# GpSimd takes over half of the scaling of the first-layer weight blocks

## The chip, the cores and the metric

The kernel runs on one core of a Trainium2 chip. A core has five engines that run side by side, each through its own fixed list of instructions: TensorE (PE in the profile, with its weight loads as PEld) multiplies matrices into PSUM; VectorE (DVE), ScalarE (ACT) and GpSimd (POOL) work on elements, 128 partitions at a time; SyncE (SP) issues most of the DMA transfers. An instruction starts when the one ahead of it on its engine has been issued and the semaphores that it waits for have been raised. The metric is the time of one execution on the device, in microseconds (us).

## What is computed

Attention with normalised queries and keys, for 8 sequences of 448 tokens and 12 heads of 64, then a layer that takes the largest of three products, and an output layer:

```python
def rmsnorm(x, g):
    rms = np.sqrt(np.mean(x * x, axis=-1, keepdims=True) + 1e-06)
    return x / rms * g
q_n, k_n = (rmsnorm(q, g_q), rmsnorm(k, g_k))
scores = (1.0 / np.sqrt(64)) * np.matmul(q_n, k_n.transpose(0, 1, 3, 2))
attn = softmax(scores)                      # rows over the keys
x = (attn @ v), heads side by side          # 3584 x 768
h = np.maximum(np.maximum(x @ w1, x @ w2), x @ w3)
out = h @ w_out                             # all weights 768 x 768
```

The weights arrive as 64-bit floats.

## The kernel before

**Products in two halves.** Most matrix products are done in f16 with each operand as a sum of an upper and a lower half: upper = f16(x), lower = f16(x - upper). Three matmuls (`TERMS`: upper by upper, upper by lower, lower by upper) give nearly the precision of f32. So that the halves use the range of f16, each operand is scaled first by a power or a bound.

**The weights.** `w1`, `w2`, `w3` are cut into 18 blocks of 128 x 768 (six column groups `ft`, three matrices `j` each), `w_out` into six. A block is loaded as raw 64-bit words (`load_raw`, two buffers) and goes through these steps, each in a later beat of the program:

- `rebias` (L188): ScalarE multiplies the upper words by a constant.
- `decode` in three stages on VectorE (L196, L200, L205): the bits of a 64-bit float become those of an f32, in place in `f`.
- when the three blocks of an `ft` are decoded, `bound_in` finds their largest magnitude (L170, then two small matmuls and a reduction in `largest`), and `scale` computes `w_up`, a column with UP / bound in each partition.
- `upper` and `lower` then split each block: this is where the change is.

`f` is no separate tile. `plain(w_sb, n)` is slot n + 1 of `w_sb` seen as f32, while the two f16 halves of block n go into slot n. So the halves of block n lie where the f32 of block n - 1 was.

**The order.** Nothing is scheduled by a tool: each engine runs its instructions in the order in which the program issues them. The program is a loop over 48 pairs of heads, `g`, with 12 beats each. A beat issues one piece of the scores, the softmax, the product with the values and the next pair's normalisation, then a few matmuls of the feed-forward layers (`thirds`), and at its end `tick()` issues what was put off to this beat by `later(beats, work)`. One first-layer block is taken up every 4 beats. `upper` of a block comes 2, 6 or 10 beats after the bound is known, `lower` 2 beats behind it. The output blocks (`bound_out`) are split in another way, which stays.

**What stands around it on the engines.** On GpSimd: the squares of queries and keys (L365), the inverse root mean squares (L383, L387), the scaling of keys and queries (L419, L423, L394, L406) and, from pair `PLAIN` = 6 on, the lower halves of queries and keys (L440) and the scaling and splitting of values (L517, L531). On ScalarE: the exponentials (L579), their preparation (L570), the copies of transposed weights (L611) and further evictions. On VectorE: the row maxima (L562), the sums of squares (L372), the lower halves of the attention weights (L665) and the decoding. The first layer's matmuls are at L732, the output layer's at L796.

Of the kernel before, what the change touches and what calls it, by code (L numbers as in the profile page):

```python
# [12 lines left out]
AF = mybir.ActivationFunctionType  # L13
ALU = mybir.AluOpType
# [25 lines left out]
def qknorm_attention_maxout_ffn_kernel(  # L40
# [35 lines left out]
    nc = tc.nc  # L76
# [36 lines left out]
    def later(beats, work, last=False):  # L113

        due.setdefault(clock[0] + beats, ([], []))[last].append(work)
# [31 lines left out]
    def largest(column, done, gaps):  # L147


        top = sb.tile([1, 1], F32, name="top", bufs=2)  # L150
        box = []

        def turn():
            box.append(ps_m.tile([P, 512], F32, name="marks", tag="m"))
            nc.tensor.matmul(box[0][0:1, 0:P], column, ident, start=True, stop=True)

        def reduce():
            nc.vector.tensor_reduce(top, box[0][0:1, 0:P], axis=AX, op=ALU.max)

        def spread():  # L160
            box.append(ps_m.tile([P, 512], F32, name="most", tag="m"))
            nc.tensor.matmul(box[1][:, 0:1], ones, top, start=True, stop=True)

        at = 0
        for gap, work in zip(gaps, (turn, reduce, spread, lambda: done(box[1][:, 0:1]))):
            at += gap
            later(at, work)

    def row_largest(dst, src):
        nc.vector.tensor_reduce(dst, src, axis=AX, op=ALU.max, apply_absolute_value=True)  # L170
# [4 lines left out]
    w_sb = const.tile([P, NFT * NJ + 1, 2, NCT * P], F16, name="w_sb")  # L175
# [55 lines left out]
    def plain(t, n):  # L231
        return t[:, n + 1].rearrange("p a n -> p (a n)").bitcast(F32)
# [17 lines left out]
    def bound_in(ft):  # L250
        most = sb.tile([P, 1], F32, name="most", bufs=2)
        n = ft * NJ + 1
        row_largest(
            most, w_sb[:, n:n + NJ].rearrange("p n a f -> p (n a f)").bitcast(F32)
        )

        def scale(bound):
            top, up = w_most[:, ft:ft + 1], w_up[:, ft:ft + 1]
            nc.vector.tensor_scalar(
                out=top, in0=bound, scalar1=LEAST, scalar2=None, op0=ALU.max  # L260
            )
            nc.vector.reciprocal(up, top)
            nc.vector.tensor_scalar(
                out=up, in0=up, scalar1=UP, scalar2=None, op0=ALU.mult
            )

            def upper(n, f):
                nc.scalar.activation(f, f, AF.Copy, scale=up)
                nc.scalar.copy(w_sb[:, n, 0], f)

            def lower(n, f):
                nc.gpsimd.tensor_tensor(
                    out=w_sb[:, n, 1], in0=f, in1=w_sb[:, n, 0], op=ALU.subtract
                )

            for j in range(NJ):
                n = ft * NJ + j
                f = plain(w_sb, n)
                later(2 + 4 * j, lambda n=n, f=f: upper(n, f), True)
                later(4 + 4 * j, lambda n=n, f=f: lower(n, f), True)  # L280

        largest(most, scale, (3, 2, 4, 1))
# [578 lines left out]
    for i, src in enumerate((g_q, g_k)):  # L861
        nc.scalar.dma_start(
            out=gains[:, i], in_=src.rearrange("(o d) -> o d", o=1).broadcast_to([P, D])
# [205 lines left out]
```

## Time and profile before

| | us |
|---|---|
| median of 3 timed runs | 1098.78 |
| lowest and highest | 1097.26, 1098.79 |
| span of the profiled execution, first to last instruction | 1101.6 |
| PE busy in that span | 1018.6 (92%) |
| DVE busy | 757.8 (69%) |
| ACT busy | 772.1 (70%) |
| POOL busy | 702.4 (64%) |
| first to last scaling of a first-layer block (L268) | 64.9 to 196.8 |
| first to last matmul of the first layer (L732) | 163.4 to 1073.9 |

The profile gives for the profiled execution its span only, and no time beside it. Shares of the whole span say little here, since the program has a stage in which weights are prepared and a longer one in which they are used. The views are read by stretches of time therefore. A group of instructions is a line with its engine and operation, how many there were, their busy time in us and the mean of one in ns, then the idle time of the engine just before them and what ended it. A row of the timeline is start and duration in us, engine, line, operation, output and inputs. The windows view gives for a stretch its length, then busy time (and instructions) of the engines, the granted clock of TensorE, the share of the DMA engines and GB/s.

### The profile page before, as it was taken

How to read it: one execution, taken by the hardware profiler on the slowest of the kernel's cores; microseconds unless marked ns; L12 is line 12 of the kernel's file. 1: busy time of each engine (PE TensorE's matmuls, PEld its weight loads, DVE VectorE, ACT ScalarE, POOL GpSimd, SP SyncE). 2: the span in 40 equal slices, each digit the busy share in tenths (PEclk: the TensorE clock that was granted, in tenths of full speed). 3: DMA queues.
4: the chain of work that ended last, by engine and by line, in shares of the span. 5: the costliest groups of instructions: out<-in, count | busy, mean ns of one | idle time of the engine just before them, and what ended most of it. 6: DMA issues, size and time to landing. Idle time of an engine off the chain costs nothing. (4 is left out here: it accounts for less than half of the span.)

```text
span 1101.6 us, 18390 instructions
## 1 busy us (share of the span) xinstructions
PE 1018.6 (92%) x6168; PEld 501.9 (46%) x6168; DVE 757.8 (69%) x1390; ACT 772.1 (70%) x1767; POOL 702.4 (64%) x805
## 2 busy tenths in 40 slices
PE   4678768988999999999999999999999999999998
PEld 2334333434444455444544454444444454445555
DVE  3899988888667676677677776777677766762210
ACT  4599887767868678687877777778777787773001
POOL 5477988856767767678677686776867677610000
PEclk9687868998989999999999999999999999999999
DMA  5554466856787679877888789787877798563002
GB/s 149 165 164 152 129 180 137 179 115 125 151 166 149 134 151 172 160 148 133 176 155 149 136 169 175 141 151 150 170 146 143 145 166 153 106 106 73 1 1 58
DMA packets 426654, 152.29 MB, mean 138 GB/s; under 512 B 372928, under 2 KB 422336, under 8 KB 426560
## 3 DMA queue, kind: packets, MB, share of 16 engines
q1 hardware_dynamic: 425888, 150.75, 66.8%
q8 instruction: 48, 0.79, 0.3%
q10 hardware_dynamic: 672, 0.38, 0.1%
q14 instruction: 46, 0.38, 0.1%
HBM read 51.97 MB, written 11.01 MB: 57 GB/s over the span
## 5 line engine op out<-in xcount | busy, mean ns | idle before, releaser
L732 PE MATMUL acc<-xt,w_sb 128*128 128x448 f16 x2592 | 520.6, 356 | 0.6 <-ACT m L742 0.6
L732 PEld LDWEIGHTS <-w_sb 128*128 128x128 f16 x2592 | 245.1, 99 | 262.9 <-issue 53.1
L562 DVE TENSOR_REDUCE sc<-sc 112x2 f32<-112x896 f32 x192 | 209.7, 1092 | 47.8 <-PE sc L553 46.6
L579 ACT ACTIVATE sc<-sc,nm,down 112x448 f32<-112x448 f32 x336 | 234.2, 697 | 11.2
L655 ACT ACTIVATE pp<-sc,rs 112x448 f16<-112x448 f32 x336 | 194.8, 632 | 48.5 <-ACT sc L579 40.4
L665 DVE SCALAR_TENSOR_TENSOR pp<-sc,rs,pp 112x448 f16<-112x448 f32 x336 | 212.9, 675 | 3.4 <-ACT pp L655 2.9
L387 POOL TENSOR_TENSOR ri<-ri,half_neg 128x7 f32<-128x7 f32 x96 | 154.2, 1606 | 8.0
L553 PE MATMUL sc<-kt,qt 64*112 64x448 f16 x1008 | 133.7, 371 | 27.1 <-DVE pp L665 23.6
L570 ACT ACTIVATE nm<-sc,down 112x2 f32<-112x2 f32 x192 | 50.7, 264 | 149.5 <-DVE sc L562 148.2
L796 PE MATMUL acc<-wo_sb,ht 128*128 128x384 f16 x864 | 151.4, 330 | 1.4 <-DVE ht L756 0.8
L761 POOL COPY hx<-ht 128x128 f16<-128x128 f16 x48 | 15.5, 323 | 197.7 <-DVE ht L756 191.7
L796 PEld LDWEIGHTS <-ht 128*128 128x128 f16 x864 | 82.0, 99 | 67.5 <-issue 14.5
L703 PE MATMUL av<-pt,vp 128*64 128x448 f16 x1008 | 108.3, 356 | 0.0
L553 PEld LDWEIGHTS <-qt 64*112 64x112 f16 x1008 | 55.0, 128 | 96.9 <-issue 56.4
L648 DVE TENSOR_SCALAR rs<-sc 112x2 f32<-112x2 f32 x168 | 26.6, 158 | 94.7 <-ACT sc L579 94.7
L440 POOL TENSOR_TENSOR kp<-kn,kp 128x512 f16<-128x512 f32 x42 | 50.0, 1190 | 58.9 <-ACT kp L434 58.9
L703 PEld LDWEIGHTS <-vp 128*64 128x64 f16 x1008 | 49.6, 108 | 56.0 <-issue 30.4
L718 DVE SCALAR_TENSOR_TENSOR xt<-av,xt 128x448 f16<-128x448 f32 x42 | 26.2, 625 | 71.1 <-ACT xt L717 71.1
L372 DVE TENSOR_REDUCE ss<-sq 128x7 f32<-128x448 f32 x96 | 60.9, 635 | 10.6 <-ACT sq L363 6.6
L531 POOL TENSOR_TENSOR vp<-vr,vp 128x448 f16<-128x448 f32 x42 | 43.8, 1044 | 32.2 <-ACT vp L525 32.1
L440 POOL TENSOR_TENSOR qp<-qn,qp 112x512 f16<-112x512 f32 x42 | 49.3, 1173 | 21.0 <-ACT qp L434 20.8
L517 POOL TENSOR_SCALAR vr<-vr,v_up 128x448 f32<-128x448 f32 x42 | 60.7, 1446 | 0.0
(112 smaller groups left out, 1203.1 us busy)
## 6 DMA issues: line engine op xcount, KB each, us to landing
raw<-in_moe_w_dram SPq DMA_DIRECT2D x18, 768.0 KB, 4.4
qr<-in_q_dram SPq DMA_DIRECT2D x48, 224.0 KB, 3.0
vr<-in_v_dram SPq DMA_DIRECT2D x96, 96.0 KB, 2.5
kr<-in_k_dram SPq DMA_DIRECT2D x95, 96.0 KB, 3.0
raw<-in_moe_w_out_dram SPq DMA_DIRECT2D x6, 768.0 KB, 5.1
pt<-pp SPq DMA_TRANSPOSE x168, 4.1
out_dram<-osb SPq DMA_DIRECT2D x8, 336.0 KB, 3.2
out_dram<-osb SPq DMA_DIRECT2D x8, 288.0 KB, 3.7
```

The lines of the kernel that those rows point to most:

```text
L372: nc.vector.tensor_reduce(sums[g % 2][:sq.shape[0], KQ[what]], sq, axis=AX, op=ALU.add)
L387: nc.gpsimd.tensor_tensor(out=ri, in0=ri, in1=half_neg[:, at], op=ALU.pow)
L440: nc.gpsimd.tensor_tensor(out=parts[:, 1], in0=n, in1=parts[:, 0], op=ALU.subtract)
L517: nc.gpsimd.tensor_scalar(out=vr, in0=vr, scalar1=v_up[:, g // NP:g // NP + 1], scalar2=None, op0=ALU.mult,)
L553: nc.tensor.matmul(sc[:QP, h, :S], qt[rows, qp, c], kt[rows, kp, KEYS[h]], start=n == 0, stop=n == len(TERMS) - 1,)
L562: nc.vector.tensor_reduce(sc[:QP, 0, S + 8:S + 10], sc[:QP, :, :S], axis=AX, op=ALU.max, negate=True)
L579: nc.scalar.activation(to, sc[:QP, h, :S], AF.Exp, bias=nm[:, h:h + 1], scale=down[:QP], accum_out=total,)
L655: nc.scalar.activation(pp[:, 0, h], sc[:QP, h, :S], AF.Copy, scale=rs[:, h:h + 1])
L665: nc.vector.scalar_tensor_tensor(out=pp[:, 1, h], in0=sc[:QP, h, :S], scalar=rs[:, h:h + 1], in1=pp[:, 0, h], op0=ALU.mult, op1=ALU.subtract,)
L703: nc.tensor.matmul(av[half, :S], vp[rows, group, vpart], pt[rows, 7 * wp + group], start=u == 0 and n == 0, stop=u == 3 and n == len(TERMS ...
L732: nc.tensor.matmul(acc[:, :S], wt[:, wp, c], xs[c][:, xp], start=(c == 0 and n == 0), stop=(c == NCT - 1 and n == 2),)
L796: nc.tensor.matmul(acc[:, :HW], lhs, wo_sb[:, f, wp, half * HW:(half + 1) * HW], start=(f == 0 and n == 0), stop=(f == NFT - 1 and n == 2),)
```

## The change

`upper` no longer scales the block in place. One ScalarE instruction reads the unscaled block, multiplies by `up` and writes the f16 upper half; the cast falls away. `lower` first scales the block in place on GpSimd, as (f x up) x 1.0, and then subtracts the upper half as before. The subtraction still needs a scaled `f`, which GpSimd now makes for itself.

```diff
             def upper(n, f):
-                nc.scalar.activation(f, f, AF.Copy, scale=up)
-                nc.scalar.copy(w_sb[:, n, 0], f)
+                nc.scalar.activation(w_sb[:, n, 0], f, AF.Copy, scale=up)
 
             def lower(n, f):
+                nc.gpsimd.tensor_scalar(
+                    out=f, in0=f, scalar1=up, scalar2=1.0, op0=ALU.mult, op1=ALU.mult
+                )
                 nc.gpsimd.tensor_tensor(
                     out=w_sb[:, n, 1], in0=f, in1=w_sb[:, n, 0], op=ALU.subtract
                 )
```

The file grows by two lines, so that lines behind the change have numbers two higher. GpSimd's list at the second, third and fourth block (`w_sb` is the block, `kn` and `qn` scaled keys and queries, `sq` squares, `ri` inverse root mean squares), before:

```order
L423 TENSOR_TENSOR kn_90<-kr,ri 64x64
L272 TENSOR_TENSOR w_sb<-w_sb 128x768
L394 TENSOR_TENSOR qn<-qr,ri 112x2x4x64
L365 TENSOR_TENSOR sq<-kr 128x448
L272 TENSOR_TENSOR w_sb<-w_sb 128x768
L365 TENSOR_TENSOR sq<-qr 112x512
L272 TENSOR_TENSOR w_sb<-w_sb 128x768
L383 TENSOR_SCALAR ri<-ss_87 128x7
```

and the same place now:

```order
L425 TENSOR_TENSOR kn_90<-kr,ri 64x64
L271 TENSOR_SCALAR w_sb<-w_sb,w_up 128x768
L274 TENSOR_TENSOR w_sb<-w_sb 128x768
L396 TENSOR_TENSOR qn<-qr,ri 112x2x4x64
L367 TENSOR_TENSOR sq<-kr 128x448
L271 TENSOR_SCALAR w_sb<-w_sb,w_up 128x768
L274 TENSOR_TENSOR w_sb<-w_sb 128x768
L367 TENSOR_TENSOR sq<-qr 112x512
L271 TENSOR_SCALAR w_sb<-w_sb,w_up 128x768
L274 TENSOR_TENSOR w_sb<-w_sb 128x768
L385 TENSOR_SCALAR ri<-ss_87 128x7
```

Ahead of each subtraction stands one more instruction; the rest keeps its order. ScalarE's list at one block (`pt` transposed weights, `nm` and `e` of the softmax), before:

```order
L611 COPY pt<-turned 128x3x112
L268 ACTIVATE w_sb<-w_sb,w_up 128x768
L269 CAST w_sb<-w_sb 128x768
L570 ACTIVATE nm<-sc,down 112x2
L579 ACTIVATE e,sum<-sc,nm,down 112x448 x2
```

and now:

```order
L613 COPY pt<-turned 128x3x112
L268 ACTIVATE w_sb<-w_sb,w_up 128x768
L572 ACTIVATE nm<-sc,down 112x2
L581 ACTIVATE e,sum<-sc,nm,down 112x448 x2
L613 COPY pt<-turned 128x4x112
```

The cast is gone, and the preparation of the softmax follows directly. The lists of TensorE, VectorE and SyncE are the same but for line numbers.

## The prediction

> **What bounds the kernel now.** First the page's second part, the busy tenths in 40 slices of 27.5 us.
>
> ```profile
> PE   4678768988999999999999999999999999999998
> DVE  3899988888667676677677776777677766762210
> ACT  4599887767868678687877777778777787773001
> POOL 5477988856767767678677686776867677610000
> ```
>
> From about slice 9 on, TensorE (PE) is busy nine tenths or more: it sets the pace, and the chain that ended last is made of its matmuls. In slices 2 to 7 (55 to 220 us) it is not: VectorE, ScalarE and GpSimd are all at seven to nine tenths. There the weight blocks are decoded, scaled and split, and only there does the change act: its rows run from 64.9 to 201 us. The order of the program is fixed, and the matmuls that follow fill TensorE almost completely, so what this stage loses or gains should shift the end by nearly as much.
>
> The windows view gives busy time per engine (PE, PEld, DVE, ACT, POOL), first for the whole stage, then slice by slice.
>
> ```profile
> 64.90:201.00 136.10, 107.05 (x566) 52.18 (x565) 123.23 (x169) 117.55 (x251) 116.01 (x98) 0.80 0.58 152
> 55.00:82.50 27.50, 20.58 (x116) 10.82 (x116) 25.79 (x36) 25.73 (x58) 19.97 (x17) 0.87 0.52 164
> 82.50:110.00 27.50, 22.71 (x109) 11.16 (x111) 27.04 (x30) 24.81 (x55) 21.86 (x18) 0.76 0.47 152
> 110.00:137.50 27.50, 20.95 (x121) 9.96 (x117) 26.04 (x31) 23.80 (x54) 24.75 (x22) 0.81 0.49 131
> 137.50:165.00 27.50, 16.97 (x84) 9.01 (x82) 24.24 (x40) 22.30 (x47) 24.41 (x22) 0.67 0.68 179
> 165.00:192.50 27.50, 24.48 (x127) 10.81 (x126) 22.64 (x37) 21.93 (x45) 22.34 (x21) 0.83 0.69 140
> 192.50:220.00 27.50, 26.27 (x159) 12.47 (x158) 23.68 (x42) 21.77 (x48) 25.02 (x24) 1.00 0.83 179
> ```
>
> In the stage's 136.1 us GpSimd is busy 116.0 and idle 20.1, ScalarE is idle 18.5, VectorE 12.9. None has room for much more.
>
> **The change part by part.** The groups of instructions in that window that it touches, and what GpSimd and VectorE waited for there:
>
> ```profile
> L272 POOL TENSOR_TENSOR w_sb<-w_sb 128x768 f16<-128x768 f32 x18 | 29.8, 1655 | 12.4 <-ACT w_sb L269 12.0
> L268 ACT ACTIVATE w_sb<-w_sb,w_up 128x768 f32<-128x768 f32 x18 | 17.1, 952 | 0.0
> L269 ACT CAST w_sb<-w_sb 128x768 f16<-128x768 f32 x18 | 15.0, 832 | 1.5
> POOL w_sb L272 <- ACT w_sb L269: 12.0, 5, 6.7
> POOL ri L383 <- DVE ss L372: 5.5, 6, 1.9
> DVE rs L648 <- ACT sc L579: 4.3, 5, 1.4
> DVE xt L718 <- ACT xt L717: 4.2, 5, 1.3
> ```
>
> *ScalarE.* Two instructions per block become one: a scaled read that writes f16. I price it between the two rows, 0.83 to 0.95 us, so 15.0 to 17.1 us of ScalarE go, over 18 blocks. That is not 15 us of time. VectorE is idle 12.9 us in the stage, and the two largest waits on ScalarE are 4.3 and 4.2; the most that ScalarE's relief can give is about those 8.5 us, while GpSimd and VectorE keep up.
>
> *GpSimd.* 18 new products over 128x768 f32, in place, stand right ahead of the 18 subtractions. No row shows this form with two operations at this size. The nearest rows, from the calmer stretch 229 to 1000 us:
>
> ```profile
> L517 POOL TENSOR_SCALAR vr<-vr,v_up 128x448 f32<-128x448 f32 x39 | 56.5, 1449 | 0.0
> L383 POOL TENSOR_SCALAR ri<-ss 128x8 f32<-128x8 f32 x37 | 7.3, 197 | 0.6 <-DVE ss L372 0.6
> L761 POOL COPY hx<-ht 128x128 f16<-128x128 f16 x39 | 11.3, 289 | 113.6 <-DVE ht L756 107.5 <-DMA kr<-in_k_dram 6.0
> ```
>
> L517 is the same operation on the same engine, with a scalar from a column, in place in f32, but with one product: 1449 ns for 448 elements. Taking the 197 ns of the 8-element row as the fixed part, an element costs (1449 - 197) / 440 = 2.85 ns, and 768 of them 0.197 + 760 x 0.00285 = 2.36 us. The other end is the one-input copy: (289 - 197) / 120 = 0.77 ns an element, 0.78 us for 768. Above, if each product costs what L517's does, 0.197 + 760 x 0.0057 = 4.5 us. I take 2.36, since L517 is the nearest row, and keep the ends. That is 18 x 2.36 = 42.5 us more on GpSimd (14.0 at the low end, 81 at the high).
>
> Against that row stands a rule of the Trainium skill, "GPSIMD Engine Reference", section 3.1, "Elementwise — side-by-side cycle accounting": a loop with at most two arithmetic operations per element is bound by its port at 1.03 cycles per element. By its 1.2 GHz that is an estimate of 0.66 us for 768 elements, plus what an instruction costs by itself; by it GpSimd would get about 15 us, not 42. L517 speaks against the rule here, at 2.85 ns or 3.4 cycles an element with only one product.
>
> Where these fall slice by slice follows from the busy time of L272 in the same windows:
>
> ```profile
> 55.00:82.50 27.50, 3.29 (x2) 0.87 0.52 164
> 82.50:110.00 27.50, 8.03 (x5) 0.76 0.47 152
> 110.00:137.50 27.50, 5.36 (x4) 0.81 0.49 131
> 137.50:165.00 27.50, 4.91 (x3) 0.67 0.68 179
> 165.00:192.50 27.50, 6.18 (x4) 0.83 0.69 140
> 192.50:220.00 27.50, 2.00 (x2) 1.00 0.83 179
> ```
>
> Divided by 1.655 us, these are 2.0, 4.9, 3.2, 3.0, 3.7 and 1.2 blocks. Times 2.36 and added to GpSimd's busy time: 24.7, 33.3, 32.4, 31.4, 31.2 and 27.9 us of work in slices of 27.5. The overflow is 0 + 5.8 + 4.9 + 3.9 + 3.7 + 0.4 = 18.7 us, with every idle moment of GpSimd in the last five slices filled. Its waits for VectorE's sums (5.5 us) can't all be filled, since the sums themselves depend on squares that GpSimd makes: I add 2. Of ScalarE's relief I count back 1, an estimate, for the first slice only, where GpSimd has room. The sum is 18.7 + 2 - 1, about 20 us.
>
> *The order on ScalarE.* One more thing follows from the layout: a block's f32 lies in the next block's slot. The f16 half of block n overwrites memory from which block n-1's subtraction reads, so ScalarE must wait for that subtraction. In the kernel before this wait stands ahead of the cast, one instruction behind the scaling; now it stands ahead of the only instruction, some 1 us sooner, and the subtraction ends later by the whole product. How close it is:
>
> ```profile
> 142.46 1.64 POOL L272 TENSOR_TENSOR w_sb<-w_sb 128x768 f16<-128x768 f32 x1
> 144.29 0.94 ACT L268 ACTIVATE w_sb<-w_sb,w_up 128x768 f32<-128x768 f32 x1
> 145.32 0.83 ACT L269 CAST w_sb<-w_sb 128x768 f16<-128x768 f32 x1
> ```
>
> The subtraction ends at 144.10, and ScalarE comes to the next block at 144.29: 0.19 us of slack, against 2.36 of delay. Behind the waiting instruction stand the exponentials and the evictions of the softmax, and TensorE and VectorE wait for those. So GpSimd's lag can't pile up quietly in the queue; it reaches all engines within a block. This is why I do not let the stage's end absorb it.
>
> *VectorE.* Its decode operations and GpSimd's keep each other out. At 81.83 the last decode step of a block (L205) waits through one GpSimd instruction and then through the next:
>
> ```profile
> 71.36 0.95 DVE L205 SCALAR_TENSOR_TENSOR w_sb<-raw,w_sb 128x768 uint32<-128x768 uint32 x1
> ...
> 80.94 1.64 POOL L365 TENSOR_TENSOR sq<-kr 128x448 f32<-128x448 f32 x1
> 81.83 3.17 DVE L205 SCALAR_TENSOR_TENSOR w_sb<-raw,w_sb 128x768 uint32<-128x768 uint32 x1
> 82.55 1.64 POOL L272 TENSOR_TENSOR w_sb<-w_sb 128x768 f16<-128x768 f32 x1
> 84.15 1.75 POOL L365 TENSOR_TENSOR sq<-qr 112x512 f32<-112x512 f32 x1
> L205 DVE SCALAR_TENSOR_TENSOR w_sb<-raw,w_sb 128x768 uint32<-128x768 uint32 x12 | 21.8, 1814 | 0.1
> 169.08 1.41 POOL L517 TENSOR_SCALAR vr<-vr,v_up 128x448 f32<-128x448 f32 x1
> 169.13 1.77 DVE L196 TENSOR_SCALAR wo_sb<-raw 128x768 uint32<-128x768 uint32 x1
> ```
>
> Free, L205 takes 0.95 us; its mean of 1.81 holds 0.86 of such waiting. The pair at 169 us shows that a product with one tensor input shuts VectorE out as well: L196 ends 0.41 us behind it. The new product makes GpSimd's run of 1.65 us one of about 4.0. If L205's wait grows in proportion, it is 0.86 x 4.0 / 1.65 = 2.1 us, 1.2 more per block and 22 over 18. I take this as the same 20 us seen from VectorE's side, not as more: while VectorE waits, GpSimd works. Only if the two add up do I get more (below).
>
> No transfer is moved; the DMAs of the next blocks hang on decoding and start later with it.
>
> **Sum.** 1101.6 (span) + 20 = 1121.6 us for a profiled execution. The median of the timed runs, 1098.78, is 2.8 us below the profiled span, so I predict 1119.
>
> **The rivals.**
> - *Cheap product, ScalarE decides* (15%): the product costs about 0.8 us as the copy does, its 14.0 us fit into GpSimd's 20.1 idle, and ScalarE's relief counts for 3 to 8.5 us: 1090 to 1096. For it: in the first two slices ScalarE is 90 to 94% busy. Against it: L517. It decides while GpSimd's time per block rises by less than its idle share of 20.1 / 18 = 1.1 us. The rule of the Trainium skill named above would lead to this case or the next.
> - *Cheap product, nothing gained* (17%): the same price, but L205's wait grows to 0.86 x 2.43 / 1.65 = 1.27, 7 us over 18, which eats the relief: 1096 to 1106.
> - *Middling product* (12%): as much as the two-input subtraction, 1.65 us. The same sum by slices overflows by 2.4 + 2.5 + 1.9 + 0.9 = 8 us: 1104 to 1111.
> - *The forecast* (44%): 1111 to 1131; the low end if ScalarE's relief of 8.5 counts in full, the high end if GpSimd's remaining waits do.
> - *Locks add up, or two products cost more than one* (12%): VectorE's 22 us stand beside GpSimd's 20, 1131 to 1141; at 4.5 us a product, 81 - 20 = 61 us, 1160.
>
> **How the numbers follow.** The range from 1093 to 1137 leaves out about half of the first and of the last case. About 0.2%, 2.2 us, is what a measurement of this kernel can tell from no change: faster is below 1096.6, slower above 1101. The first case gives 0.14 faster, the second splits into 0.08 same and the rest slower; with a little kept back on either side that is 0.15, 0.10 and 0.75.
>
> **What the profile of the changed kernel would show.** The price of a product, in its own group: 2.4 us carries the forecast, 0.8 a cheap-product rival. GpSimd at over 95% busy from 82 to 200 us, hardly a wait for ScalarE left. ScalarE idle ahead of its scaled cast, waiting for the subtraction of the block before. L205 above 2 us. The stage some 20 us longer, with the first layer's matmuls starting some 14 us later (the overflow up to 165 us), and nothing changed behind it. I am wrong if the product is short, or if the stage is longer and TensorE wins it back afterwards.

## The result, and the profile after

| | before | after |
|---|---|---|
| median of the timed runs, us | 1098.26 (4 runs) | 1106.49 (4 runs) |
| span of the profiled execution, us | 1101.6 | 1105.7 |

The ratio is 1.0073, with a 95% interval from 1.0057 to 1.0089: the change makes the kernel slower by 8 us. I had forecast 1119, and my range began at 1093, so the time lies inside the range and the direction is right; the 20 us of the forecast are 8. The granted clock doesn't explain the longer time: in the profiled executions its mean was 0.957 before and 0.966 after.

The page's busy tenths after the change:

```profile
PE   4687747988989999999999999999999999999998
...
DVE  4799968888767676677677766777677767762210
ACT  4587757768777778687777777777777787773001
POOL 5479999966676777767677686776867677620000
```

In slices 3 to 7 GpSimd (POOL) now has nines throughout, where it had 7 to 9 before; ScalarE (ACT) fell. From slice 10 on little has changed. The windows view of the stage and of its slices (columns as before):

```profile
64.90:201.00 136.10, 99.14 (x541) 48.99 (x540) 119.11 (x163) 99.05 (x223) 129.57 (x110) 0.82 0.53 143
82.50:110.00 27.50, 19.36 (x100) 10.07 (x99) 25.33 (x30) 20.40 (x47) 26.70 (x21) 0.75 0.49 152
110.00:137.50 27.50, 21.13 (x121) 9.59 (x122) 25.92 (x30) 21.85 (x51) 26.71 (x22) 0.87 0.45 132
137.50:165.00 27.50, 13.87 (x81) 7.96 (x77) 18.66 (x32) 17.06 (x39) 26.66 (x24) 0.75 0.48 137
165.00:192.50 27.50, 21.02 (x102) 9.32 (x104) 24.88 (x41) 20.15 (x45) 26.74 (x25) 0.88 0.79 167
```

From 82 to 192 us GpSimd is busy 97% of the time, and every other engine is less busy than before in most of these slices. The new product, the wait that it causes and the decode steps, taken from the line's own view, the groups of the stage and the waits in it:

```profile
L271 POOL TENSOR_SCALAR w_sb<-w_sb,w_up x18: 896/905/2292, 66.2 to 205.7; 128x768 f32<-128x768 f32 x18
L271 POOL TENSOR_SCALAR w_sb<-w_sb,w_up 128x768 f32<-128x768 f32 x17 | 19.3, 1136 | 6.7 <-ACT w_sb L268 6.0
ACT w_sb L268 <- POOL w_sb L274: 16.8, 7, 5.0
L205 DVE SCALAR_TENSOR_TENSOR w_sb<-raw,w_sb 128x768 uint32<-128x768 uint32 x12 | 14.6, 1220 | 0.1
L200 DVE SCALAR_TENSOR_TENSOR w_sb<-raw,w_sb 128x768 uint32<-128x768 uint32 x12 | 16.7, 1388 | 0.1
L734 PE MATMUL acc<-xt,w_sb x2592: 349/352/581, 169.5 to 1078.0; 128*128 128x448 f16 x200
```

The first three numbers of a line's view are the shortest, median and longest duration in ns. A product takes 905 ns in the median and 1136 in the mean of the stage, where I had put 2360. By the timeline 14 of the 18 take 0.90 or 0.91 us; the two that start while VectorE's decode step L205 is running (at 83.62 and 154.34) take 1.60, and two more 2.07 and 2.29. ScalarE waits 16.8 us for the subtraction of the block before; in the kernel before it was idle for 1.5 us ahead of its 18 casts. The first layer begins at 169.5 us instead of 163.4 and ends at 1078.0 instead of 1073.9. One of ScalarE's waits in the timeline:

```profile
101.80 2.22 POOL L274 TENSOR_TENSOR w_sb<-w_sb 128x768 f16<-128x768 f32 x1
...
104.05 0.94 ACT L268 ACTIVATE w_sb<-w_sb,w_up 128x768 f16<-128x768 f32 x1 [3.74 <-POOL w_sb L274]
```

GpSimd ends a subtraction at 104.02, and ScalarE, which had been ready 3.74 us before, starts the next block at 104.05. What stands behind it in ScalarE's list, the softmax above all, had to wait with it.

### The profile page after: what moved, and what is told of

Same layout as the page of the kernel before. It is cut to its first block, busy times and chain, and to the rows that moved or that the text cites. A ratio compares the mean times of both kernels' runs of the same rounds, so it can differ in the third digit from the quotient of the medians.

```text
span 1105.7 us, 18378 instructions
## 1 busy us (share of the span) xinstructions
PE 1011.9 (92%) x6168; PEld 499.8 (45%) x6168; DVE 756.8 (68%) x1390; ACT 757.6 (69%) x1749; POOL 722.3 (65%) x823
```

## The experiments

Three questions: was the price of the product the only thing wrong; does the cost come through GpSimd's filled list (theory A) or through ScalarE's wait at the head of its queue (theory B); and why does ScalarE's relief of some 15 us bring nothing to set against it? Each run was timed beside the kernel before on the same chip; I compare ratios, since the medians of the kernel before lie between 1098.3 and 1099.6 in these sets. The profiled spans scatter by several us against the medians, so the verdicts go by the timed runs.

**Price and dose.** The product with one operation:

```diff
-    out=f, in0=f, scalar1=up, scalar2=1.0, op0=ALU.mult, op1=ALU.mult
+    out=f, in0=f, scalar1=up, scalar2=None, op0=ALU.mult
```

> The changed kernel with GpSimd's product written with one operation instead of two, the form of the existing scaling of the values. If the one-operation form costs an element what it costs there, 2.85 ns, a product takes about 2.3 us instead of 0.9 and GpSimd gets 18 x 1.45 = 26 us more. Theory A, and the recorded sum: 1116 to 1122 us against before. Theory B: the wait of ScalarE grows by at most 1.45 us at each of 7 to 11 places, 1114 to 1122 as well; the pair tells the price apart from the mechanism, not A from B. If the form doesn't matter: as the changed kernel, 1105 to 1108 us.

Measured: 1118.35 us, ratio 1.0169 (1.0146 to 1.0193). Its line and its largest wait:

```profile
L271 POOL TENSOR_SCALAR w_sb<-w_sb,w_up x18: 2198/2211/3379, 65.4 to 216.2; 128x768 f32<-128x768 f32 x18
ACT w_sb L268 <- POOL w_sb L274: 29.8, 11, 6.3
```

The one-operation form takes 2.21 us (2.41 on the mean of the stage), near the 2.36 of the forecast, and the time is that of the forecast within 1 us. The form with a second, idle product is the cheaper one, by a factor of 2.4.

The product written twice (the second by 1.0 and 1.0, right behind the first):

```diff
+    nc.gpsimd.tensor_scalar(
+        out=f, in0=f, scalar1=1.0, scalar2=1.0, op0=ALU.mult, op1=ALU.mult
+    )
```

> The changed kernel with a second product, by 1.0 and 1.0, behind the first: GpSimd gets 18 x 0.95 = 17 us more. Theory A: GpSimd is filled, so nearly all of it lengthens the stage, 1118 to 1124 us. Theory B: ScalarE waits about 1 us longer at 7 to 11 places, 1113 to 1118 us. If there is still slack: 1108 to 1112 us.

Measured: 1117.79 us, ratio 1.0165 (1.0140 to 1.0191). Both forms of more load on GpSimd end at about the same time: 2.21 us of product, or 0.91 and a median of 1.01. Per us put on GpSimd, some 0.4 to 0.5 us of time come out, by the means in the stage: 18 x 1.14 = 20 us gave 8, 18 x (1.14 + 1.09) = 40 gave 18.1, 18 x 2.41 = 43 gave 18.6. The value lies in theory B's range at its upper end, and just below A's; it decides nothing between them.

**ScalarE's wait and GpSimd's load.** The f32 of a block two slots ahead of its halves instead of one, so that the scaled cast has nothing to wait for (the last block's f32 lies in the first slot of the output weights, which is free until then):

```diff
-    w_sb = const.tile([P, NFT * NJ + 1, 2, NCT * P], F16, name="w_sb")
-    wo_sb = const.tile([P, NFT + 1, 2, DO], F16, name="wo_sb")
+    both = const.tile([P, NFT * NJ + 1 + NFT + 1, 2, NCT * P], F16, name="w_sb")
+    w_sb, wo_sb = both, both[:, NFT * NJ + 1:]
...
-        return t[:, n + 1]...
+        return t[:, n + (2 if t is w_sb else 1)]...
...
-        n = ft * NJ + 1
+        n = ft * NJ + 2
```

> The changed kernel with each block's f32 two slots ahead of its f16 halves instead of one, so that ScalarE's scaled cast overwrites the f32 of the block before the last and no longer waits for GpSimd's latest subtraction (16.8 us of such waits in the changed kernel); instruction lists are otherwise the same. Theory A, GpSimd's filled queue sets the stage's length: the waits only move to other engines, and the time stays at 1104 to 1108 us. Theory B, the wait at the head of ScalarE's queue is what costs: the 8 us go and ScalarE's relief shows, 1092 to 1099 us.

Measured: 1102.62 us, ratio 1.0030 (1.0016 to 1.0045). It falls between both theories: more than half of the cost goes, but not all. The waits in its stage show where the rest can be (two lines of this run, then one of the changed kernel):

```profile
DVE ss L374 <- POOL sq L367: 7.4, 4, 3.9
ACT qp L436 <- POOL qn L408: 6.5, 2, 3.3
...
DVE ss L374 <- POOL sq L367: 0.3, 1, 0.3
```

VectorE now stands before its sums of squares, because GpSimd comes late with the squares; in the changed kernel it waited 0.3 us there. ScalarE, freed from the wait at the scaled cast, now waits 6.5 us for scaled queries, for which it had not waited at all. Take one wait for GpSimd away, and others appear.

The other half, GpSimd's load taken away: the squares of the first ten pairs on ScalarE, which has room in the changed kernel.

```diff
-        if g < 2:
+        if g < 10:
             nc.scalar.activation(sq, src, AF.Square)
```

> The changed kernel with the same squares on ScalarE, which there has the room that the change made. GpSimd loses 12 of the 17 to 20 us that the product gave it. Theory A, GpSimd's filled queue makes the 8 us: 1098 to 1102 us. If the 8 us come from something that doesn't hang on GpSimd's load: 1105 to 1108 us.

Measured: 1101.71 us, ratio 1.0029 (1.0017 to 1.0041): again some 5 of the 8 us, as theory A has it. Both at once:

> The changed kernel with the f32 two slots ahead, so that ScalarE doesn't wait for GpSimd, and the squares of the first ten pairs on ScalarE, so that GpSimd has its load of before: nothing of the computation is left out. If the 8 us are ScalarE's wait and GpSimd's load and nothing else, none of them is left: 1097 to 1100 us. Below 1096 if ScalarE's remaining relief counts, above 1101 if a part of the cost lies elsewhere.

Measured: 1098.12 us, ratio 0.9988 (0.9975 to 1.0001). Nothing of the cost is left. The cost is GpSimd's lateness, and it can be reduced at its source or where it is handed on, each time by somewhat more than half. The product itself, and its meetings with VectorE's decode steps, are still there; by themselves they cost nothing that shows. Beside the kernel before this is no gain that the interval confirms.

Two controls. The squares on ScalarE in the kernel before, and the new place of the blocks in the kernel before:

> The kernel before with the squares of the pairs up to the tenth on ScalarE (0.57 and 0.62 us there for keys and queries) instead of GpSimd (0.93 and 1.04): in the stage GpSimd loses some 6 x 2 = 12 us, ScalarE gets 6 x 1.2 = 7 us. If GpSimd and the port set the pace even before: 1091 to 1097 us. If VectorE's own work does, or ScalarE has no room for 7 us more: 1098 to 1103 us.

> The kernel before with the f32 two slots ahead: its cast no longer waits for the subtraction of the block before, which it hardly does (ScalarE idles 1.5 us ahead of all 18 casts). Any theory: 1097 to 1099 us. More would mean that the new place of the blocks costs by itself.

Measured: 1097.57 us, 0.9995 (0.9985 to 1.0005), and 1098.29 us, 0.9990 (0.9974 to 1.0005). Both change nothing; the first lies between the two ranges that I had given. It is telling: in the stage GpSimd's busy time falls from 116.0 to 106.9 us, ScalarE's grows from 117.6 to 124.1, and this brings nothing; after the change the same move brings 5 us.

**What ScalarE's relief is worth.** The kernel before with GpSimd's product alone (by 1.0 and 1.0), ScalarE's two instructions as they were:

```diff
+    nc.gpsimd.tensor_scalar(
+        out=f, in0=f, scalar1=1.0, scalar2=1.0, op0=ALU.mult, op1=ALU.mult
+    )
     nc.gpsimd.tensor_tensor(
```

> The kernel before with a product of two operations, by 1.0 and 1.0, on GpSimd ahead of each subtraction: GpSimd's load of the change without ScalarE's relief. Theory A, GpSimd's filled queue sets the length and ScalarE's relief is worth nothing: as the changed kernel, 1104 to 1108 us. If the relief gives back a part behind the filled queue: 1109 to 1113 us. If most of the 8 us comes from ScalarE's earlier wait (its first instruction of a block now waits for the subtraction of the one before, instead of its second): 1100 to 1104 us.

Measured: 1106.74 us, ratio 1.0068 (1.0044 to 1.0091): the changed kernel's time. The added product makes the whole of the loss, with or without the relief. ScalarE's wait in it, now again ahead of the cast:

```profile
ACT w_sb L269 <- POOL w_sb L275: 8.1, 5, 4.1
```

It is half of the changed kernel's 16.8 us, and the time of the whole is the same: the earlier place of the wait brings no loss that shows beside the relief. And the relief without the product, then without any wait on GpSimd as well (two slots):

```diff
-    nc.gpsimd.tensor_scalar(
-        out=f, in0=f, scalar1=up, scalar2=1.0, op0=ALU.mult, op1=ALU.mult
-    )
```

> The changed kernel without GpSimd's product (the lower half is made from the unscaled block): ScalarE has one instruction per block as in the change, GpSimd has what it had before. It prices ScalarE's relief alone. Theory A: GpSimd keeps 20 us idle as before, the relief counts for the waits of VectorE and TensorE on ScalarE, 1088 to 1096 us. Theory B with an earlier wait on ScalarE (about 1 us sooner than before, the subtraction ends no later): 1092 to 1099 us. If the relief is worth nothing: 1097 to 1099 us.

> The kernel without the product (the lower half is made from the unscaled block) and with the f32 two slots ahead: ScalarE's relief alone, without any wait on GpSimd. If ScalarE's relief is worth nothing because VectorE and the port it shares with GpSimd set the pace: 1098 to 1101 us, as without the product. If the earlier wait on GpSimd ate the relief: 1091 to 1097 us.

Measured: 1100.6 us, 1.0013 (1.0001 to 1.0025), and 1100.63 us, 1.0017 (1.0005 to 1.0029). The first is above all three ranges that I had given, the second is in the range for VectorE. The relief alone gives nothing, if anything a loss of 1 to 2 us, for which I have no cause, and the earlier wait isn't what eats it. Where the relief went stands in the stage's windows row without the product, and in the waits of ScalarE with two slots and, last, in the kernel before:

```profile
64.90:201.00 136.10, 102.73 (x558) 49.68 (x555) 124.91 (x170) 102.78 (x232) 117.05 (x98) 0.82 0.57 153
...
ACT nm L569 <- DVE sc L561: 21.5, 10, 3.7
...
ACT nm L570 <- DVE sc L562: 6.8, 4, 2.4
```

ScalarE is busy 102.8 instead of 117.6 us, VectorE 124.9 instead of 123.2, and ScalarE now waits 21.5 us for VectorE's row maxima, which was 6.8 before. The freed time became waiting for VectorE.

Is VectorE then the engine that sets the pace? Product and subtraction as one instruction on VectorE, which empties GpSimd:

```diff
-    nc.gpsimd.tensor_scalar(...)
-    nc.gpsimd.tensor_tensor(...)
+    nc.vector.scalar_tensor_tensor(
+        out=w_sb[:, n, 1], in0=f, scalar=up, in1=w_sb[:, n, 0],
+        op0=ALU.mult, op1=ALU.subtract,
+    )
```

> The changed kernel with product and subtraction as one instruction on VectorE, as the output blocks have it: GpSimd loses 18 x (0.9 + 1.65) us, VectorE gets 18 x about 1.0. If GpSimd's queue and the port that both use set the pace: faster than before, 1085 to 1094 us. If VectorE's own busy time does (123 of 136 us in the stage): 1100 to 1112 us.

Measured: 1104.01 us, ratio 1.0041 (1.0029 to 1.0052). Slice by slice:

```profile
82.50:110.00 27.50, 19.18 (x123) 9.28 (x119) 27.40 (x34) 20.91 (x49) 16.46 (x14) 0.94 0.47 150
110.00:137.50 27.50, 20.44 (x90) 9.78 (x89) 27.40 (x34) 19.74 (x46) 19.34 (x16) 0.69 0.46 129
...
POOL ri L383 <- DVE ss L372: 30.5, 8, 4.8
```

VectorE is busy 27.4 of 27.5 us, and GpSimd, with room to spare, waits 30.5 us for its sums. The opposite way, a list of VectorE made shorter: the kernel before without the third decode step of the first-layer blocks, and the same without product and with two slots.

```diff
-        for stage in range(3):
+        for stage in range(2 if kind == "in" else 3):
```

> The kernel before without the third decode step of the first-layer blocks (their lowest three bits are left out): VectorE loses 18 instructions of 0.95 us, 1.8 with their waits, and so does the port. If VectorE, by itself or through the port, sets the pace of the stage: 1080 to 1091 us. If GpSimd's or ScalarE's lists do: 1094 to 1099 us.

> ScalarE's relief alone (no product, f32 two slots ahead), and the first-layer blocks' third decode step left out as well. Against the run with the short decode alone it prices ScalarE's relief when VectorE is no longer full. If ScalarE comes next: 5 to 10 us below that run. If the relief is worth nothing here either: within 2 us of it.

Measured: 1094.18 us, 0.9967 (0.9951 to 0.9984), and 1087.96 us, 0.9907 (0.9885 to 0.9928). The first is less than I had expected, and just inside the range for the lists of GpSimd or ScalarE: VectorE's relief counts for 4 us, so VectorE isn't the only limit, and then ScalarE is the next one. With VectorE shorter, ScalarE's relief, worth nothing alone, is worth 6 to 7 us.

So the changed kernel with the short decode, with one slot, with two, and with the squares on ScalarE:

> The changed kernel without the third decode step of the first-layer blocks (their lowest three bits are left out). Against the same short decode on the kernel before (1094.2 us) it says what the change is worth when VectorE is no longer full. If GpSimd's filled queue makes the cost by itself: it stays slower than that, 1095 to 1103 us. If the cost came from GpSimd and VectorE shutting each other out, and ScalarE's relief now counts: 1088 to 1094 us.

> The changed kernel with the f32 two slots ahead and without the third decode step of the first-layer blocks. With one slot it took 1095.4 us, without product and with two slots 1088.0. If most of the product's cost reaches the end through ScalarE's wait, as the first set says (product 6 to 7 us with that wait, 1 to 2 without): 1088 to 1091 us. If the cost is GpSimd's load by itself: 1093 to 1096 us.

> The same with the squares of the first ten pairs on ScalarE: GpSimd's load is nearly that of before, ScalarE keeps about half of its relief, VectorE has its relief. If each engine's list counts as soon as it is the fullest, all three are now shorter or equal: 1088 to 1093 us, below the kernel before and the changed one. If GpSimd's product still costs: 1094 to 1099 us.

Measured: 1095.43 us, 0.9963 (0.9952 to 0.9975); 1095.75 us, 0.9963 (0.9944 to 0.9982); 1091.49 us, 0.9937 (0.9914 to 0.9960). The first lies at the lower edge of the range for GpSimd's filled queue, but by its ratio it equals the short decode on the kernel before (0.9967): here ScalarE's relief and GpSimd's product cancel. The second refutes what the first set had made me believe, that the product costs little once ScalarE doesn't wait for it. It costs 0.9963 - 0.9907, 6 us, with no wait at ScalarE's scaled cast; VectorE waits for the squares instead, and ScalarE for scaled queries:

```profile
64.90:201.00 136.10, 105.32 (x595) 51.95 (x595) 109.05 (x168) 107.44 (x241) 132.24 (x120) 0.87 0.59 155
...
DVE ss L374 <- POOL sq L367: 7.5, 3, 2.7
ACT qp L436 <- POOL qn L408: 4.2, 2, 2.1
```

GpSimd is busy 132.2 of 136.1 us there. The third is below both kernels, with three bits of the first-layer weights left out; among the runs that leave nothing out, none is clearly faster than the kernel before.

**The cheap form elsewhere.** The scaling of the values in the kernel before, as two products:

```diff
-            out=vr, in0=vr, scalar1=v_up[:, g // NP:g // NP + 1], scalar2=None,
-            op0=ALU.mult,
+            out=vr, in0=vr, scalar1=v_up[:, g // NP:g // NP + 1], scalar2=1.0,
+            op0=ALU.mult, op1=ALU.mult,
```

> The kernel before with GpSimd's scaling of the values (448 elements, 1.41 us) written as two products, like the change's: by the element price of the change's product, (905 - 197) / 760 = 0.93 ns, it should take 0.197 + 440 x 0.00093 = 0.61 us. 42 of them, 34 us of GpSimd's time, but only some three in the stage in which GpSimd is short: 1095 to 1098 us if those count, 1098 to 1099 if nothing does.

Measured: 1098.8 us, 0.9991 (0.9979 to 1.0004). The form behaves as expected, but the time doesn't change:

```profile
L517 POOL TENSOR_SCALAR vr<-vr,v_up x42: 637/642/1334, 169.3 to 977.7; 128x448 f32<-128x448 f32 x42
```

642 ns instead of 1410, 32 us less on GpSimd over the kernel, and nothing of it shows: GpSimd is not what is waited for there.

## Why the prediction was right or wrong

*The price of the product: wrong, and the mis-sized term of the sum.* I took 2.36 us from the scaling of the values, which has one operation, and kept 0.78 from the copy as the other end. It is 0.905 us, 1.14 in the mean of the stage, so 18 products put 20 us on GpSimd and not 42.5. With the price that I had taken, the forecast holds: the one-operation form measured 2.21 us and 1118.35, against 1119. The row of L383, from which I took the fixed part, does have two operations, but at 8 elements it shows nothing of their price. From 448 to 768 elements, the two-operation form costs (905 - 642) / 320 = 0.82 ns an element, the one-operation form (2211 - 1410) / 320 = 2.50. The rule of the Trainium skill in "GPSIMD Engine Reference", section 3.1 (1.03 cycles an element), fits the form that was used: by its 1.2 GHz, 0.82 ns are an estimate of 0.99 cycles. It doesn't fit the form with one operation, at an estimate of 3.0 cycles. I had set a row with another form above it.

*The sum by slices: good at the large price, wrong at the small one.* It counted only what overflows GpSimd's slices. At 2.41 us a product it gives 19 us, and 18.6 were measured. With 1.14 us it would have given about 1 us: 21.9 + 4.9 x 1.14 just reaches 27.5, and the other slices overflow by 0.9, 0.3 and 0. Measured are 8. So the right price alone would not have saved the forecast: with it the same sum says about 1101. The two errors pull in opposite directions, and that the sum fits at the large price is no proof of its rule. Idle time of GpSimd was not free room: 12.0 of its 20.1 idle us before were waits for ScalarE's cast, and while neither ScalarE nor VectorE had waited for it in the stage, they do once it is filled. The three loads that were run, 20, 40 and 43 us, cost 0.4 to 0.5 us per us added; a smaller one by itself was not run.

*The order on ScalarE: right.* The wait for the subtraction of the block before appeared, 16.8 us, with the softmax behind it, and taking it away recovers 4 to 5 of the 8 us. It is one of the ways by which GpSimd's lateness travels, not the only one (VectorE's sums and ScalarE's copies of the queries are others): with the short decode, taking it away brings nothing (1095.43 and 1095.75). And the 1 us by which it came sooner makes no difference that shows: the product alone in the kernel before costs as much.

*ScalarE's relief worth little: right, and more so than put.* I allowed at most 8.5 us. By itself it is worth nothing, since ScalarE then waits for VectorE; it is worth 6 to 7 us when VectorE's list is shorter. I had read ScalarE's 90 to 94% in the first slices as a limit; VectorE's 94 to 98% there was the harder one.

*VectorE and GpSimd keeping each other out: wrong in size and sign.* I had L205 at above 2 us. It fell from 1.81 to 1.22, and L200 rose from 1.14 to 1.39; the two together became shorter by 0.35 us. The mean wait didn't grow with the length of GpSimd's run. That it hangs on where the two lists meet is likely, but no run shows it. Nor does a product always shut VectorE out, as I had read from the pair at 169 us. The row of L200 before, and then two rows of the run with one operation:

```profile
L200 DVE SCALAR_TENSOR_TENSOR w_sb<-raw,w_sb 128x768 uint32<-128x768 uint32 x12 | 13.7, 1140 | 0.1
...
101.86 2.51 POOL L271 TENSOR_SCALAR w_sb<-w_sb,w_up 128x768 f32<-128x768 f32 x1
103.14 0.55 DVE L196 TENSOR_SCALAR w_sb<-raw 128x768 uint32<-128x768 uint32 x1
```

L196 took 0.55 us in the middle of that product, against 1.77 in the pair at 169 us.

*The rivals.* At the cheap price the time was to be 1090 to 1106, and 1106.5 is just above the worse of these two cases. But that case's reason, a longer wait of L205, is not what happened. The faster case failed because ScalarE's relief by itself is worth nothing. The time does lie in the range of the middling product, 1104 to 1111, but by luck: that case has 1.65 us a product, all of it overflow, and neither is so.

*The end.* I expected TensorE to win nothing back. The profiled pair starts the first layer 6.1 us later, where I had put 14, and ends it 4.1 us later; the timed medians are 8.2 apart. Profiled spans of single executions scatter too much here to say more.

## What to carry to other kernels

In this kernel three engines are each 85 to 91% busy in lists of fixed order. Relieving one moved the waiting to the next, while loading another cost 8 us although its idle time could nearly hold the load. To find the engine that the others wait for, relieve one engine at a time and look whose waits grow: here ScalarE's relief turned into waits for VectorE and began to count when VectorE was relieved too. And take the price of an operation from a row of the very same form: a second operation, idle, changed it by a factor of 2.4.

## What the runs showed of the hardware that was not expected

GpSimd's product of a tensor with a column, 128x768 in f32, takes 2.21 us with one operation and 0.905 us with two, the second by 1.0; for 128x448 it is 1.41 and 0.642 us. Why the form with more operations is the shorter one, no run shows. With both scalars constant, the shortest was 0.82 us (the line of the product alone in the kernel before):

```profile
L272 POOL TENSOR_SCALAR w_sb<-w_sb x18: 821/830/1536, 65.0 to 205.1; 128x768 f32<-128x768 f32 x18
```
